# Batch 2's first matmul in seven products, a two-bank end and a searched table of priority shifts in a linear attention plus MLP kernel

## The chip, the cores and the metric

The kernel runs on one core of one Trainium2 chip. The time is the device time of one execution in microseconds. A core has five engines, each with its own instruction queue: TensorE (PE, matmuls; PEld is its weight load), VectorE (DVE), ScalarE (ACT), GpSimd (POOL) and SyncE (SP). Transfers are issued from the queues of SP, POOL and ACT and run on 16 DMA engines. A queue is worked off in its order, so an instruction that waits holds all those behind it.

## What is computed

The reference is a linear attention over 8 batches, 8 heads, 576 positions and head width 64, followed by an MLP with a squared ReLU over all 4608 tokens (512 to 2048 to 512). Inputs and output are float32.

```python
pos = np.arange(S)
theta = np.pi / 2.0 * pos / S
def phi(x, c, s):
    r = np.maximum(x, 0.0)
    return np.concatenate([r * c, r * s], axis=-1)
q_p, k_p = phi(q, cos_w, sin_w), phi(k, cos_w, sin_w)
kv = np.einsum('bhsf,bhsd->bhfd', k_p, v)
z = np.sum(k_p, axis=2)
num = np.einsum('bhsf,bhfd->bhsd', q_p, kv)
den = np.einsum('bhsf,bhf->bhs', q_p, z)[..., None] + 1e-06
x = (num / den).transpose(0, 2, 1, 3).reshape(B * S, H * D)
h = x @ w_in
g = np.maximum(h, 0.0) ** 2
out = g @ w_out
```

## The kernel before

**Batches and tails.** A batch has 576 positions: four groups of 128 (j = 0 to 3, J = 4) and a tail of 64. The MLP works on nine blocks m of 512 tokens: m = 0 to 7 are the four full groups of a batch, and m = 8 holds the eight tails. The first matmul (x times w_in) has 16 row blocks hb of 128 hidden units, the second (g times w_out) sums over them.

**The attention of a batch.** DVE or ACT make the features of k (`plan_k`), cast v (`plan_v`) and make those of q (`plan_q`); L278 and L282 are one such operation on ACT and on DVE, L300 and L302 the casts. PE multiplies k and v into the pair of banks abank (L324), one copy takes that to kvz (L335). The q features are transposed by a DMA that SP issues (L348) or, in batches 0 and 1, by PE (L357). PE makes numerator and denominator (L375), DVE divides (`att_div`, L393 to L399), and the result x is transposed into xT, two groups j at a time, by a DMA of SP (L416) or by PE (L421).

**The seven products.** Both matmuls can be done as a product of 2 x 2 block matrices with seven block products instead of eight, with sums and differences of blocks (the Winograd form). For the second matmul this is so for every batch but the first: sums of w_out's blocks are made once (L665, into w2t), sums of g's blocks per batch (`g_sum`, L684, into gs), and `product` (L705) issues each block product as two halves (sub 0 and 1) of eight matmuls of 256 columns. For the first matmul it is so from batch FIRST_7 on (L1152: 3). There `w1_sum` (L495) makes four sums of w_in's blocks once, w1t; one of them is written over a block of w_in, so it must come behind the last plain matmul. `x_sum` (L519) makes four differences of xT's blocks per batch into the buffers xs; `in_product` (L537) issues a block product as four matmuls of 256 columns. Four lanes u cover the hidden units, alternately on banks 0 and 1 and on banks 2 and 3 (`LANES`, L521). In each lane ACT copies product 5 aside (L933), seeds one bank with the contents of the other (L916, twice) and does two ReLUs (L553), DVE adds product 5 to two results (`in_add`, L560), takes their maximum with zero (L577), and squares the lane (L477).

**The plain first matmul.** In batches 1 and 2 (`plan_gemm1`) each of the 16 hb is four matmuls of 512 columns (L460; for three of batch 1's, L444 in two halves of 256) and one ReLU on ACT (L469); DVE squares four hb at a time (L477). Batch 0 has its own code (L585, L595, L604, L610).

**The order.** `Plan` holds every step from batch 0's first matmul on, with its engine or engines, cost, due time and lag. `order` derives a due time for each step from those that depend on it (L62 to L68), and then fills the engines greedily: each free engine takes, of the steps that are ready in the plan's own clock, the one with the earliest due time (L87). The result is a fixed sequence per engine. A step that lists DVE and ACT is given to either. `plan_load`, `plan_qT` and `plan_x` add the loads and the transposes of SP's queue. The loads of batches 0 and 1 and of the weights stand outside the plan.

**The end.** Block 8's second matmul uses banks 0 (X), 1 (Y), 5 (Z) and 4 (V), L1029. `last` writes a result block to ysb by ACT (L994) or, with product 5 added, by DVE (L990), and `store_half` stores it with two DMAs (L639). The last product, 4, adds onto bank Z; then two ACT copies, one for each half (`last_copy`, L650), and four stores of 64 KB (`put_quarter`, L647), three issued from SP and one from ACT.

Of the kernel before, what the change touches and what calls it, by code (L numbers as in the profile page):

```python
# [13 lines left out]

EPS = 1e-06
FP = 512


class Plan:
# [10 lines left out]
    def add(self, eng, dur, fn, r=(), w=(), due=None, lag=None, name="", after=0.0):  # L30


        n = len(self.ops)
        deps = set()
        for key in r:
            if key in self.last_write:
                deps.add(self.last_write[key])
        for key in w:
            if key in self.last_write:
                deps.add(self.last_write[key])  # L40
            deps.update(self.readers.get(key, ()))
        at = max([self.given.get(key, 0.0) for key in (*r, *w)] + [after])
        for key in r:
            self.readers.setdefault(key, set()).add(n)
        for key in w:
            self.last_write[key] = n
            self.readers[key] = set()
            self.given.pop(key, None)
        if isinstance(eng, str):
            eng, dur, fn = (eng,), (dur,), (lambda e, f=fn: f())  # L50
        lag = self.LAG[eng[0]] if lag is None else lag
        self.ops.append([eng, dur, fn, deps, due, lag, at, name])
        return n

    def order(self, t0):
        ops = self.ops
        n = len(ops)
        after = [[] for _ in range(n)]
        for i, op in enumerate(ops):
            for d in op[3]:  # L60
                after[d].append(i)
        due = [0.0] * n  # L62
        for i in reversed(range(n)):
            eng, dur, _, _, own, lag, _, _ = ops[i]
            t = own if own is not None else 1e6
            for s in after[i]:
                t = min(t, due[s] - min(dur) - lag)
            due[i] = t  # L68
        left = [len(op[3]) for op in ops]
        ready = [op[6] for op in ops]  # L70
        free = {"PE": t0, "ACT": t0, "DVE": t0, "POOL": t0, "SP": t0}
        waiting = {e: [] for e in free}
        for i in range(n):
            if not left[i]:
                for e in ops[i][0]:
                    waiting[e].append(i)
        done, self.by = [], {}
        self.start, self.due = [0.0] * n, due
        while len(done) < n:
            best = None  # L80
            for e, some in waiting.items():
                if some:
                    s = max(free[e], min(ready[i] for i in some))
                    if best is None or s < best[0]:
                        best = (s, e)
            s, e = best
            i = min((i for i in waiting[e] if ready[i] <= s + 0.02), key=lambda i: (due[i], i))  # L87
            s = max(s, ready[i])
            for other in ops[i][0]:
                waiting[other].remove(i)  # L90
            self.by[i] = e
            dur, lag = ops[i][1][ops[i][0].index(e)], ops[i][5]
            free[e] = s + dur
            self.start[i] = s
            done.append(i)
            for a in after[i]:
                left[a] -= 1
                ready[a] = max(ready[a], s + dur + lag)
                if not left[a]:
                    for o in ops[a][0]:  # L100
                        waiting[o].append(a)
        return sorted(done, key=lambda i: (self.start[i], i))
# [7 lines left out]
def kernel(  # L110
# [9 lines left out]
    nc = tc.nc  # L120
# [596 lines left out]
    def half_bank(to):  # L717
        return bank[to][:, :].rearrange("p (s c) -> p s c", s=2)
# [81 lines left out]
    def q_parts(js):  # L800
        return [qp_key(j) + (x,) for j in js for x in "cs"]

    def plan_qT(b, i):
        js = (2 * i, 2 * i + 1) if i < J // 2 else (J,)
        add("SP", 2.0 if i < J // 2 else 1.5, lambda: att_qT(b, i), r=q_parts(js),
            w=[("qpT", i)], lag=CARE + (2.4 if i < J // 2 else 1.7))
        for j in js:
            where[b, j] = ("qpT", i)
# [12 lines left out]
    def x_key(j):  # L821
        return ("xt",) if j == J else ("x", j)
# [6 lines left out]
    def plan_x(b, i):  # L829
        js = (2 * i, 2 * i + 1) if i < J // 2 else (J,)  # L830
        w = [("xT", b % 2, j) for j in js] if i < J // 2 else [("xT8", b // 2)]
        if i < J // 2:
            add("SP", 1.3, lambda: att_x(b, i), r=[x_key(j) for j in js], w=w, lag=1.7 + CARE)
        else:
            add("SP", 1.2, lambda: att_x(b, i), r=[x_key(j) for j in js], w=w, lag=1.7 + CARE)

    def plan_x_pe(b, j, to, due, eng):
        add("PE", 4 * 0.057, lambda: att_x_pe(b, j, to), r=[x_key(j)], w=[("bank", to)], due=due)
# [131 lines left out]
    def plan_gemm2(m, t, dt):  # L970
        hs = range(HB2)
        g = lambda i, j: g_keys(m, i, j, hs)
        s = lambda n: [("gs", n, h) for h in hs]
        reads = {1: g(0, 0), 2: g(0, 1), 5: s(1), 6: s(2), 7: g(1, 0), 3: s(4), 4: g(1, 1)}
        c = [0]

        def prod(n, to):
            for sub in range(2):
                add("PE", 8 * 0.1092, lambda sub=sub: product(m, n, sub, to), r=reads[n] + [("w2t", n, c2) for c2 in range(2)],
                    w=[("bank", to)], due=t + c[0] * dt, name=f"p{m}.{n}.{sub}")  # L980
                c[0] += 1

        def seed(a, b):
            add("ACT", cost("ACT", 512, "psum"), lambda: nc.scalar.copy(out=bank[b][:, :], in_=bank[a][:, :]),
                r=[("bank", a)], w=[("bank", b)])

        def last(a, i, cc, five):
            if five:
                add("DVE", cost("DVE", 512, "psum"),
                    lambda: nc.vector.tensor_tensor(out=y_view(m, i, cc), in0=half_bank(a), in1=five_of(m)[:, :, :], op=ALU.add),  # L990
                    r=[("bank", a), ("five",)], w=[("y", y_slot(m, i), cc)])
            else:
                add("ACT", cost("ACT", 512, "psum"),
                    lambda: nc.scalar.copy(out=y_view(m, i, cc), in_=half_bank(a)),  # L994
                    r=[("bank", a)], w=[("y", y_slot(m, i), cc)])
# [13 lines left out]

        if m < B:  # L1010
            X, Y = 4, 5
            prod(1, X)
            prod(5, Y)
            five(Y)
            seed(X, Y)
            prod(6, Y)
            prod(2, X)
            last(X, 0, 0, False)
            seed(Y, X)
            prod(7, X)  # L1020
            prod(3, Y)
            last(X, 1, 1, True)
            last(Y, 0, 1, True)
            store(0)
            prod(4, X)
            last(X, 1, 0, False)
            store(1)
            return
        X, Y, Z, V = 0, 1, 5, 4  # L1029
        prod(1, X)  # L1030
        seed(X, Y)
        prod(2, X)
        last(X, 0, 0, False)
        store_half(0, 0, ("POOL", "POOL"))
        prod(6, Y)
        seed(Y, Z)
        prod(5, V)
        five(V)
        prod(7, Z)
        last(Z, 1, 1, True)  # L1040
        store_half(1, 1, ("POOL", "POOL"))
        prod(3, Y)
        last(Y, 0, 1, True)
        store_half(0, 1, ("SP", "SP"))
        prod(4, Z)
        for sub in range(2):
            add("ACT", cost("ACT", 256, "psum"), lambda sub=sub: last_copy(sub, Z),
                r=[("bank", Z)], w=[("y", 1, 0, sub)])
            for g, q in enumerate(("SP", "ACT") if sub else ("SP", "SP")):
                add(q, 0.6, lambda g=g, q=q, sub=sub: put_quarter(1, ENG[q], g, sub, 0, DM2),  # L1050
                    r=[("y", 1, 0, sub)], w=[("out", m, 1, 0, g, sub)])

# [96 lines left out]
    t = tB + 4.0  # L1149
    dC = 0.98  # L1150
    win[0] = (t, t + 14.0)
    FIRST_7, STRIDE, SHIFT = 3, 2.0, -6.0  # L1152
    if FIRST_7 == 1:
        plan_w1_sums(28.0)
        plan_gemm1_7(1, t, 0.5)
# [120 lines left out]
```

## Time and profile before

| | |
|---|---|
| median of 3 runs | 281.94 us (280.93 to 282.44) |
| profiled execution | 282.92 us, of which the span is 281.1 us |
| granted TensorE clock | 0.999 |
| HBM read, written | 36.70 MB, 9.44 MB |
| DVE squares L477 | 32 instructions, 38.0 us busy |
| plain ReLUs L469 on ACT | 32 instructions, 18.9 us busy |
| seeds L916 and copies of product 5, L933, on ACT | 48 and 24 instructions, 27.8 and 14.2 us |
| out stores of 512 KB from SP | 16, 4.0 us from issue to landing |

The profile is one execution. Its span goes from the first to the last instruction; 1.8 us of the device time lie around it. PE's instructions overlap in their ends, so where times are added the chain of waits and the distances of starts are used rather than the mean length of one matmul (273 ns for 256 columns, at a distance of 109).

```profile
DVE  1567775899998959698999999998799869949901
ACT  3575962987957875599997997965555553675220
DMA  6999999899999999989999999292033100300224
```

These are the 40 slices of the span: the tenths in which DVE, ACT and the DMA engines were busy. The transfers fill the first 60% of the span and then thin out.

### The profile page before, as it was taken

What the parts mean: (1) busy time and instruction counts of PE and PEld (TensorE: products, weight loads), DVE (VectorE), ACT (ScalarE), POOL (GpSimd) and SP (SyncE); (2) the same over time, 40 slices, a digit from 0 to 9 for tenths busy, and PEclk for the clock granted to TensorE, in tenths of its full rate; (3) what the DMA queues carried; (4) which work ended last, traced back from release to release, by engine and by line L of the source; (5) the groups of instructions that cost most, each with busy time, mean ns of one, the idle gap of its engine ahead of it and who ended that gap; (6) DMA issues with size and microseconds to landing.
All of it is one profiled execution on the core that took longest, in us unless ns stands there. A gap on an engine that the chain in (4) does not pass through costs nothing.

```text
span 281.1 us, 6673 instructions
## 1 busy us (share of the span) xinstructions
PE 267.1 (95%) x2702; PEld 214.5 (76%) x2707; DVE 224.4 (80%) x442; ACT 185.5 (66%) x330; POOL 18.2 (6%) x31
## 2 busy tenths in 40 slices
PE   8599999999799989998999999999999999999993
PEld 3378965565466658897889898998898888888882
DVE  1567775899998959698999999998799869949901
ACT  3575962987957875599997997965555553675220
POOL 8427000000000000000000000000000000000011
PEclk9999999999999999999999999999999999999999
DMA  6999999899999999989999999292033100300224
GB/s 216 312 206 293 315 225 365 234 241 340 280 179 280 256 193 235 332 221 216 323 209 323 201 253 263 43 231 106 2 74 116 55 2 0 152 0 2 111 79 112
DMA packets 83566, 53.38 MB, mean 190 GB/s; under 512 B 55888, under 2 KB 79952, under 8 KB 83536
## 3 DMA queue, kind: packets, MB, share of 16 engines
q1 hardware_dynamic: 77472, 42.41, 58.8%
q0 software_dynamic: 5984, 10.49, 15.8%
q8 instruction: 21, 0.34, 0.5%
q14 instruction: 9, 0.07, 0.1%
q10 hardware_dynamic: 80, 0.07, 0.1%
HBM read 36.70 MB, written 9.44 MB: 164 GB/s over the span
## 4 chain that ended last, share of the span: by engine, by line
PE 79%; DMA 10%; DVE 5%; issue 1%; POOL 1%; SPq 1%; ACT 1%; POOLq 0%; DVEq 0%
PE bank L705 30%; PE bank L537 24%; PE bank L460 6%; PE bank L610 5%; PE bank L585 5%; DMA xT<-x 5%; PE abank L324 3%; DMA q<-in_q_dram 3%; PE abank L375 3%; DMA v<-in_v_dram 2%; PE bank L357 1%; DVE gT L477 1%; SPq L176 1%; PE bank L444 1%; PE bank L421 1%
## 5 line engine op out<-in xcount | busy, mean ns | idle before, releaser
L705 PEld LDWEIGHTS <-gT 128*128 128x128 bf16 x512 | 49.5, 98 | 7.2 <-DVE gT L477 0.3
L705 PE MATMUL bank<-w2sb,gT 128*128 128x256 bf16 x384 | 49.8, 273 | 0.0
L553 ACT ACTIVATE gT<-bank 128x512 bf16<-128x512 f32 x48 | 28.4, 600 | 31.4 <-PE bank L537 30.8
L477 DVE TENSOR_TENSOR gT<-gT 128x2048 bf16<-128x2048 bf16 (+1 forms) x32 | 38.0, 1188 | 7.9 <-ACT gT L553 6.7
L537 PE MATMUL bank<-xT,w1sb 128*128 128x256 bf16 x288 | 42.4, 273 | 1.4 <-DMA xT<-x 1.4
L537 PEld LDWEIGHTS <-w1sb 128*128 128x128 bf16 x384 | 36.8, 98 | 6.6 <-DMA xT<-x 2.0
L705 PEld LDWEIGHTS <-gs 128*128 128x128 bf16 x384 | 37.1, 98 | 6.2 <-DVE gs L684 1.4
L560 DVE TENSOR_TENSOR gT<-bank,qpTp 128x512 bf16<-128x512 f32 x48 | 32.1, 685 | 6.9 <-PE bank L537 5.0
L705 PE MATMUL bank<-w2t,gs 128*128 128x256 bf16 x256 | 33.2, 273 | 0.8 <-DVE gs L684 0.7
L537 PEld LDWEIGHTS <-w1t 128*128 128x128 bf16 x288 | 27.1, 98 | 4.5 <-DVE qpTp L519 1.2
L537 PE MATMUL bank<-qpTp,w1t 128*128 128x256 bf16 x192 | 28.3, 273 | 0.8 <-DVE qpTp L519 0.8
L460 PE MATMUL bank<-xT,w1sb 128*128 128x512 bf16 x116 | 27.8, 379 | 1.3 <-DMA xT<-x 1.3
L916 ACT COPY bank<-bank 128x512 f32<-128x512 f32 x48 | 27.8, 588 | 0.5
L469 ACT ACTIVATE gT<-bank 128x512 bf16<-128x512 f32 x32 | 18.9, 596 | 9.8 <-PE bank L460 9.5
L399 DVE TENSOR_TENSOR x<-abank,rden 128x512 bf16<-128x512 f32 x31 | 21.4, 691 | 1.1
L460 PEld LDWEIGHTS <-w1sb 128*128 128x128 bf16 x116 | 10.5, 98 | 11.5 <-DMA xT<-x 1.6
L639 POOL DMA_DIRECT2D out_dram<-ysb x4 | 2.4, 617 | 245.4 <-ACT ysb L994 242.2
L933 ACT COPY qpTp<-bank 128x512 f32<-128x512 f32 x24 | 14.2, 598 | 5.2 <-PE bank L537 5.0
L705 PE MATMUL bank<-w2sb,gs 128*128 128x256 bf16 x128 | 16.6, 273 | 0.0
L705 PE MATMUL bank<-w2t,gT 128*128 128x256 bf16 x128 | 16.5, 273 | 0.0
L990 DVE TENSOR_TENSOR ysb<-bank,y 128x512 f32<-128x512 f32 x16 | 11.0, 685 | 6.8 <-PE bank L705 6.6
L994 ACT COPY ysb<-bank 128x512 f32<-128x512 f32 x15 | 8.8, 588 | 11.2 <-PE bank L705 10.9
(101 smaller groups left out, 431.7 us busy)
## 6 DMA issues: line engine op xcount, KB each, us to landing
out_dram<-ysb SPq DMA_DIRECT2D x16, 512.0 KB, 4.0
v<-in_v_dram SPq DMA_DIRECT2D x12, 512.0 KB, 6.9
q<-in_q_dram SPq DMA_DIRECT2D x12, 512.0 KB, 5.3
k<-in_k_dram SPq DMA_DIRECT2D x12, 512.0 KB, 6.5
v<-in_v_dram POOLq DMA_DIRECT2D x2, 1024.0 KB, 12.6
w1sb<-in_moe_w_in_dram POOLq DMA_DIRECT2D x4, 512.0 KB, 12.7
w2sb<-in_moe_w_out_dram POOLq DMA_DIRECT2D x4, 512.0 KB, 15.3
k<-in_k_dram SPq DMA_DIRECT2D x1, 1024.0 KB, 5.4
```

What stands on the lines that cost most here:

```text
L399: nc.vector.tensor_tensor(out=x[:, a:z], in0=n4[:, :, :, 0:D].rearrange("p b (k l) d -> p b k l d", l=2), in1=rden[:, a:z] .rearrange("p b ...
L460: nc.tensor.matmul(out=out_, lhsT=w1sb[:, kb, hb * P : (hb + 1) * P], rhs=x_block(m, kb), start=(kb == 0), stop=(kb == KB - 1),)
L469: nc.scalar.activation(out=gT_of(m)[:, hb, :], in_=bank[to][:, :], func=ACTF.Relu)
L477: nc.vector.tensor_tensor(out=g, in0=g, in1=g, op=ALU.mult)
L537: nc.tensor.matmul(out=bank[to][:, s * W : (s + 1) * W], lhsT=lhs[:, kb, (2 * u + s) * P : (2 * u + s + 1) * P], rhs=rhs[:, kb, :], start= ...
L553: nc.scalar.activation(out=g_pair(m, i, j, u), in_=bank[to][:, :].rearrange("p (s c) -> p s c", s=2), func=ACTF.Relu,)
L560: nc.vector.tensor_tensor(out=g_pair(m, i, j, u), in0=bank[to][:, :].rearrange("p (s c) -> p s c", s=2), in1=in_five(u).rearrange("p (s c) ...
L585: nc.tensor.matmul(out=bank[2 * (s % 2) + i // 2][:, i % 2 * W + c : i % 2 * W + c + step], lhsT=w1sb[:, kb, hb * P : (hb + 1) * P], rhs=x ...
L610: nc.tensor.matmul(out=bank[FIRST_Y[tt]][:, :], lhsT=gT_of(0)[:, hb, tt * P : (tt + 1) * P], rhs=w2sb[:, hb, :], start=(hb == 0), stop=(hb ...
L705: nc.tensor.matmul(out=bank[to][:, s * DM2 : (s + 1) * DM2], lhsT=lhs[:, hb, s * P : (s + 1) * P], rhs=rhs[:, hb, :], start=(fresh and hb ...
L916: add("ACT", psum, lambda: nc.scalar.copy(out=bank[b][:, :], in_=bank[a][:, :]), r=[("bank", a)], w=[("bank", b)])
L933: add("ACT", psum, lambda u=u, Y=Y: nc.scalar.copy(out=in_five(u), in_=bank[Y][:, :]), r=[("bank", Y)], w=five)
```

## The change

Three things are changed.

1. FIRST_7 goes from 3 to 2: batch 2's first matmul is done in seven products, and w_in's block sums (`plan_w1_sums`) may start from the plan's time 28 on.
2. In the end of block 8, bank Z is copied by ACT in two halves into banks 2 and 3 after product 7. The first half of product 4 adds onto bank 2 and the second onto bank 3. Each half is copied to ysb and stored when it is done: the first by two stores from POOL, the second by one from SP and one from ACT.
3. The planner adds a number from the table SHIFTS (306 entries, from -12.6 to 12.8) to the due time of a step, by the step's number. Between two steps that only PE can do, the lag is taken as zero (`behind`). The costs of four of SP's transposes in the plan are raised.

```diff
+SHIFTS = {
+    40: -2.8, 60: -2, 72: -3.8, 74: -2.4, 78: 4, 92: -1.2, 126: -1.4, 137: 1.2, 145: 7.4, 147: 2.2,
...
+    1128: 0.2, 1130: -4.8, 1131: -1.4, 1137: -1.6, 1139: 0.2, 1140: -2, 1194: 1, 1199: -7.6,
+}
...
+    def behind(self, i, a):
+
+        return 0.0 if self.ops[i][0] == self.ops[a][0] == ("PE",) else self.ops[i][5]
+
     def order(self, t0):
...
             for s in after[i]:
-                t = min(t, due[s] - min(dur) - lag)
-            due[i] = t
+                t = min(t, due[s] - min(dur) - self.behind(i, s))
+            due[i] = t + SHIFTS.get(i, 0.0)
...
-                ready[a] = max(ready[a], s + dur + lag)
+                ready[a] = max(ready[a], s + dur + self.behind(i, a))
...
-        add("SP", 2.0 if i < J // 2 else 1.5, lambda: att_qT(b, i), r=q_parts(js),
+        add("SP", 2.3 if i < J // 2 else 1.6, lambda: att_qT(b, i), r=q_parts(js),
             w=[("qpT", i)], lag=CARE + (2.4 if i < J // 2 else 1.7))
...
-            add("SP", 1.3, lambda: att_x(b, i), r=[x_key(j) for j in js], w=w, lag=1.7 + CARE)
+            add("SP", 1.7, lambda: att_x(b, i), r=[x_key(j) for j in js], w=w, lag=1.6 + CARE)
         else:
-            add("SP", 1.2, lambda: att_x(b, i), r=[x_key(j) for j in js], w=w, lag=1.7 + CARE)
+            add("SP", 1.4, lambda: att_x(b, i), r=[x_key(j) for j in js], w=w, lag=1.7 + CARE)
...
         prod(7, Z)
         last(Z, 1, 1, True)
         store_half(1, 1, ("POOL", "POOL"))
+
+        for sub in range(2):
+            add("ACT", cost("ACT", 256, "psum"),
+                lambda sub=sub: nc.scalar.copy(out=half_bank(2 + sub)[:, sub, :], in_=half_bank(Z)[:, sub, :]),
+                r=[("bank", Z)], w=[("bank", 2 + sub)])
         prod(3, Y)
         last(Y, 0, 1, True)
         store_half(0, 1, ("SP", "SP"))
-        prod(4, Z)
         for sub in range(2):
-            add("ACT", cost("ACT", 256, "psum"), lambda sub=sub: last_copy(sub, Z),
-                r=[("bank", Z)], w=[("y", 1, 0, sub)])
-            for g, q in enumerate(("SP", "ACT") if sub else ("SP", "SP")):
+            add("PE", 8 * 0.1092, lambda sub=sub: product(m, 4, sub, 2 + sub), r=reads[4] + [("w2t", 4, c2) for c2 in range(2)],
+                w=[("bank", 2 + sub)], due=t + c[0] * dt, name=f"p{m}.4.{sub}")
+            c[0] += 1
+            add("ACT", cost("ACT", 256, "psum"), lambda sub=sub: last_copy(sub, 2 + sub),
+                r=[("bank", 2 + sub)], w=[("y", 1, 0, sub)])
+            for g, q in enumerate(("SP", "ACT") if sub else ("POOL", "POOL")):
                 add(q, 0.6, lambda g=g, q=q, sub=sub: put_quarter(1, ENG[q], g, sub, 0, DM2),
                     r=[("y", 1, 0, sub)], w=[("out", m, 1, 0, g, sub)])
...
-    FIRST_7, STRIDE, SHIFT = 3, 2.0, -6.0
+    FIRST_7, STRIDE, SHIFT = 2, 2.0, -6.0
```

More of the change, by code (lines that the diff above doesn't have):

```diff
@@ L63, in order @@
         for i in reversed(range(n)):
-            eng, dur, _, _, own, lag, _, _ = ops[i]
+            _, dur, _, _, own, _, _, _ = ops[i]
             t = own if own is not None else 1e6
             for s in after[i]:
-                t = min(t, due[s] - min(dur) - lag)
-            due[i] = t
+                t = min(t, due[s] - min(dur) - self.behind(i, s))
+            due[i] = t + SHIFTS.get(i, 0.0)
         left = [len(op[3]) for op in ops]
@@ L91, in order @@
             self.by[i] = e
-            dur, lag = ops[i][1][ops[i][0].index(e)], ops[i][5]
+            dur = ops[i][1][ops[i][0].index(e)]
             free[e] = s + dur
```

32 rows, old and new, of the table SHIFTS are left out of this document.

## The prediction

> **What bounds the kernel now.** I read the busy shares first, then the same by stage, then what TensorE (PE) waited for, then the last microseconds.
>
> ```profile
> PE 267.1 (95%) x2702; PEld 214.5 (76%) x2707; DVE 224.4 (80%) x442; ACT 185.5 (66%) x330; POOL 18.2 (6%) x31
> L460 PE MATMUL bank<-xT,w1sb 128*128 128x512 bf16 x116 | 27.8, 379 | 1.3 <-DMA xT<-x 1.3
> ...
> L560 DVE TENSOR_TENSOR gT<-bank,qpTp 128x512 bf16<-128x512 f32 x48 | 32.1, 685 | 6.9 <-PE bank L537 5.0
> ```
>
> PE is busy for 95% of the span. The L460 row is the plain first matmul in 512-wide pieces: 64 of its 116 are batch 2's, which the change replaces; the L560 row is one of the vector operations that seven products bring along.
>
> ```profile
> core 0: us, PE busy (x) PEld busy (x) DVE busy (x) ACT busy (x) POOL busy (x), PEclk, DMA share, GB/s
> 36.00:55.00 19.00, 18.79 (x172) 10.79 (x174) 12.99 (x33) 10.94 (x20) 0.00 (x0) 1.00 1.01 267
> 55.00:70.00 15.00, 15.00 (x140) 8.59 (x138) 14.65 (x30) 11.59 (x21) 0.00 (x0) 1.00 1.07 296
> 70.00:84.00 14.00, 11.99 (x119) 7.61 (x118) 13.61 (x28) 10.48 (x20) 0.00 (x0) 1.00 1.09 233
> 84.00:112.00 28.00, 26.54 (x249) 18.96 (x247) 23.46 (x47) 20.60 (x37) 0.00 (x0) 1.00 1.09 243
> 112.00:140.00 28.00, 27.09 (x312) 23.85 (x311) 24.02 (x48) 23.91 (x44) 0.00 (x0) 1.00 0.95 268
> 140.00:168.00 28.00, 28.00 (x302) 24.85 (x300) 27.16 (x55) 25.15 (x46) 0.00 (x0) 1.00 1.10 253
> 168.00:196.00 28.00, 28.00 (x321) 25.16 (x319) 26.74 (x53) 19.61 (x37) 0.00 (x0) 1.00 0.67 162
> ```
>
> Columns after the stretch: its length, then the busy time of each engine. PE is full in 55:70 and from 140 on. From 70 to 140 it stands still for 2.01, 1.46 and 0.91 us. VectorE (DVE) is nearly full in 55:84 (28.3 of 29), but only at 84% in 84:112.
>
> ```profile
> PE bank L537 <- DMA xT<-x: 1.4, 2, 0.9
> PE bank L460 <- DMA xT<-x: 1.3, 1, 1.3
> PE bank L537 <- DVE qpTp L519: 0.8, 1, 0.8
> PE bank L705 <- DVE gs L684: 0.7, 1, 0.7
> ```
>
> These are the waits behind the idle time: late transposed inputs xT, and late DVE sums (gs, and the input differences of L519).
>
> ```profile
> 103.56 0.61 PE L537 MATMUL bank<-qpTp,w1t 128*128 128x256 bf16 x4 [0.75 <-DVE qpTp L519]
> ```
>
> This is the first product of batch 3 that needs an input difference; it is my mark for how far each kernel has come.
>
> ```profile
> 274.58 1.91 PE L705 MATMUL bank<-w2t,gT 128*128 128x256 bf16 x16
> 276.52 0.65 ACT L650 COPY ysb<-bank 128x256 f32<-128x256 f32 x2 [4.78 <-PE bank L705]
> 276.92 1.78 SPq L647 DMA_DIRECT2D out_dram<-ysb  x3
> 277.20 0.56 ACTq L647 DMA_DIRECT2D out_dram<-ysb  x1
> ```
>
> The last product ends at about 276.49; then two ACT copies, four small stores, and the end at 281.1.
>
> **The base.** The sum is made against the profiled execution: 282.92 us, of which 281.1 are the span and 1.8 lie around it. It stands 0.98 above the median of the runs, 281.94. I carry a change of the span onto that median.
>
> **Batch 2 in seven products, on PE.** 64 matmuls of 512 columns become 112 of 256. In the chain of waits four of the first kind take 0.865 us, eight of the second 0.873: 64 x 0.216 = 13.83 against 112 x 0.109 = 12.23, so -1.6.
>
> Every 256-wide matmul also needs its weight load, of which there are 48 more. The loads' mean is 98 ns, yet the last 128 matmuls of the chain take 14.11 us, 110 ns each, so they lie wholly beside the matmuls. The Trainium skill (TensorE: Matmul & The Clock Gate, The mechanism) says that loads overlap matmuls only where row groups differ; all these use all 128 rows, so by that rule 48 x 0.098 = 4.7 us would be added and the part would cost 3.1. The trace disagrees.
>
> **On ACT and DVE.** Batch 2's sixteen ACT relus (L469, about 0.6) become eight relus, eight seed copies (L916) and four copies of product 5 (L933): +4 x 0.6 = 2.4 us on an engine at 20.6 of 28; hidden. DVE gets eight L560 (starts 0.61 apart), four maxima (0.35) and four L519 (0.34): +7.6 us. The four weight sums of L495 (1.13 each), which stood between 81.7 and 106.3, go forward: in the built order one stands behind the squares at about 27, two about the v casts at 39 to 41. DVE was idle 1.08 us up to 28.6 and 4.34 us up to 44.9, so these three cost nothing; without that cover they would cost 3.4. The fourth must wait for the last plain unit of batch 1 and lands at about 73, where DVE has no slack. As cover, several feature operations (0.40 each) go from DVE to ACT: between the sums of batch 1 and those of batch 2, DVE has 13 features and casts where it had 19.
>
> **DVE up to batch 1's sums.** In the old kernel the second half of the first sum (L684) is done at 73.16. The new order puts before it one more feature (0.40) and the fourth weight sum (1.13), and takes out a cast (0.34): +1.2. The attention matmuls of batch 1, which these wait for, stand behind about 0.6 us more of L610 work: 75.0. PE had product 1 of batch 1 finished at 71.99, and now does 0.87 of batch 2 before it needs the sum: 72.9, a wait of 2.1. Before it waited 0.71 + 1.31 = 2.02 here. A wash, but the place has a new owner: DVE in place of the transposed input.
>
> That input is not gone. In the old queue two 512 KB stores stood ahead of its second half, which was issued at 70.11 and landed 5.9 us later. Now the stores follow it and one v load precedes it. With 3.5 us (the median of these transposes) to 5.9 us it lands 74.2 to 76.6, counted from 70.7; its difference is wanted at 75.0. Cost 0 to 1.6, I take 0.5. Behind it on DVE all four differences queue, and with them six of the seven products.
>
> **From there to the mark.** DVE's list from 75.0 through the first difference of batch 3, by the distances of starts in its timeline: seven feature operations 2.8; three casts 1.0; five attention divisions 5.2 (1.04 each); eight L560 4.9; four maxima 1.4; four squares of 2048 4.6; eight half sums L684 4.8; two output sums 1.2; five differences 1.7: 27.6. PE after its wait has 3.1 of work up to batch 2's second products (78.1), then 200 matmuls of 256 and 88 of 65 columns (0.0306 each), 24.5, so 102.6: DVE decides. It is never quite full. In 140:196, where the same mix runs, its share is 53.9 of 56, 96%: 27.6 / 0.96 = 28.75, and the mark is reached at 103.75. Before: 103.56. But behind the mark the old order has 1460 matmuls of 256 and 320 of 65, the new 1432 and 320. So 28 x 0.109 - 0.2 = 2.9 us gained: the 1.6, and the old PE's waits of 0.60 (at 98.4, for batch 3's xT) and 0.75 (at the mark itself), which a PE that arrives with DVE does not have.
>
> **Behind the mark.** Old idle time there: 0.85 (xT, at 129) and 0.13. The whole order is new, and each new neighbourhood can open a wait; in 140:262 there was none to win. Bounds: -1.0 (those two gone) to +1.5 (as much as 84:112 shows, once). I take +0.7.
>
> **The end.** L650's two copies waited for all 16 matmuls of product 4; now the first follows the first eight and only one copy (0.375) is behind the last. Before, SP issued its third quarter store at 278.2, 1.71 after the product's end; the new last ones, from SP and ACT, start 0.03 + 0.375 + 0.03 = 0.44 after it: -1.27. POOL's two (0.62 each to issue) begin 0.4 before the product's end, the second 0.2 after; its stores took 2.3 to 3.1 us to land against 2.3 of SP's: at worst the gain is 0.7. New are two ACT copies that seed the banks, about 0.65, behind product 7 and beside product 3 (1.75); if they come after DVE's read of that bank (0.75) the cover is 0.15. I take -1.0, bounds -0.7 to -1.3.
>
> For POOL's stores the Trainium skill (DMA: Bandwidth & Descriptors, Anatomy of one DMA) has 2.0 us plus bytes / 436e3, for 64 KB an estimate of 2.15; with that the end would gain 1.15. No row here shows a 64 KB store from POOL.
>
> **Sum.** -2.9 + 0.5 + 0.7 - 1.0 = -2.7: 281.94 - 2.7 = 279.2 us. The planner's other edits (no lag between two PE steps, longer costs of SP's transposes) add no instruction; they act through the order alone.
>
> **Rivals.** *Everything fits* (0.15): no new wait behind the mark, none for xT, PE rather than DVE reaches the mark, 1.1 earlier: -2.9 - 1.1 - 1.0 - 1.0 = -6.0, 275.9. For it: the idle time is there to be filled. Against: DVE was never over 98% in any stage.
>
> *DVE with small gaps* (0.13): 90% in place of 96% gives 27.6 / 0.90 = 30.7, +1.9: 281.1. For it: 84:112 and 112:140 ran at 84 and 86%, though they partly waited for DMA.
>
> *DMA sets the pace* (0.10): its share is 0.95 to 1.10 up to 168. If batch 4's xT still lands at 129.4, the 2.9 turns into waiting there and only the end stays: 280.9. Against: the chain shows these transposes released by DVE's division.
>
> *DVE becomes the bound* (0.19), the one on the other side: between 75 and 104 DVE and PE wait for each other in turn (division for attention matmul, product for a bank that L560 reads). At the 84% of the old 84:112 the list takes 32.9: +4.1, so 283.3, and with xT and later waits at their upper bounds 285.2; call it 284.2. It decides from a share under 88%, where 2.7 is used up. For it: 7.6 us more DVE work in a stage without cover. Against: the stretches 55:84 and 140:196 hold 96 to 97%.
>
> *Weight loads are not hidden* (0.01), by the loads' mean of 98 ns: -2.7 + 4.7, 283.9; every 256-wide row speaks against it.
>
> **How the numbers follow.** The forecast has 0.42; its own range, from its bounds without all of them at one end, is 277.6 to 280.9. Over 0.5% (1.4 us, about what a measurement of this kernel can tell from no change) faster: 0.36 of it, 0.15, and 0.07 of the two middle rivals: 0.58. Slower: 0.16 of the fourth and 0.02: 0.18. The rest, 0.24, is the same. The range reaches down most of the way to the first rival and up into the fourth: 276.8 to 283.6.
>
> **What would show it.** PE's waits: a DVE wait of about 2 us for gs near 73 and at most 0.5 for xT; no L495 among them. DVE at 95% or more from 75 to 104, and batch 3's first difference product at 102.6 to 104.5. After the last product one ACT copy and about 3.6 us to the end, not 4.6. Wrong, if PE waits over 2 us in total behind 140, if DVE falls below 88% between 75 and 104, or if the seeds hold up product 4.

## The result and the profile after

| | before | after |
|---|---|---|
| median | 282.19 us (280.93 to 283.53, 4 runs) | 278.99 us (278.64 to 279.47, 4 runs) |
| profiled execution | 282.92 us, span 281.1 | 279.47 us, span 277.7 |

The ratio is 0.988, with a 95% interval of 0.983 to 0.992: 3.2 us faster. The forecast was 279.2. (Ratios here and below leave disturbed runs out, while medians don't; in e4 below, with three such runs of six, the two therefore differ.)

The lines of the changed kernel stand 43 further down: L705, L537, L519, L495 and L684 are now L748, L580, L562, L538 and L727. First PE, DVE and the others by stage, with the columns of before:

```profile
core 0: us, PE busy (x) PEld busy (x) DVE busy (x) ACT busy (x) POOL busy (x), PEclk, DMA share, GB/s
70.00:84.00 14.00, 11.87 (x139) 9.28 (x137) 13.90 (x29) 14.00 (x26) 0.00 (x0) 1.00 0.93 233
84.00:112.00 28.00, 26.54 (x300) 23.42 (x299) 25.97 (x53) 25.08 (x46) 0.00 (x0) 1.00 1.11 232
112.00:140.00 28.00, 28.00 (x313) 25.23 (x313) 26.48 (x54) 22.49 (x41) 0.00 (x0) 1.00 1.03 246
```

PE still stands still for 2.13 us in 70:84 (2.01 before) and for the same 1.46 us in 84:112. Only the 0.91 us of 112:140 are gone. What it waited for (the waits of PE: total, times, longest):

```profile
PE bank L748 <- DVE gs L727: 1.9, 1, 1.9
PE bank L580 <- DMA xT<-x: 1.5, 1, 1.5
```

The first is the new wait for batch 1's sums, the second is again a transposed input, now batch 3's first half. In PE's timeline it stands ahead of the product of 98.87, and the mark, the first product of batch 3 that takes a difference, follows at 105.63:

```profile
98.87 0.61 PE L580 MATMUL bank<-xT,w1sb 128*128 128x256 bf16 x4 [1.46 <-DMA xT<-x]
...
105.63 0.60 PE L580 MATMUL bank<-qpTp,w1t 128*128 128x256 bf16 x4
```

DVE between the sums of batch 1 and the mark (same columns as the stages): 27.44 of 29 us, 95%. Its first difference for batch 3 starts at 104.06.

```profile
75.00:104.00 29.00, 27.00 (x314) 23.27 (x315) 27.44 (x57) 26.39 (x49) 0.00 (x0) 1.00 1.06 240
```

The end, in the timeline: the two seeds, product 4 in its two banks, the first copy while the second half runs, POOL's two stores, the second copy, the last two stores.

```profile
270.31 0.63 ACT L1088 COPY bank<-bank 128x256 f32<-128x256 f32 x2 [1.07 <-DVE ysb L1033]
...
271.08 1.91 PE L748 MATMUL bank<-w2t,gT 128*128 128x256 bf16 x16
...
272.15 0.37 ACT L693 COPY ysb<-bank 128x256 f32<-128x256 f32 x1 [1.20 <-PE bank L748]
272.81 1.07 POOL L690 DMA_DIRECT2D out_dram<-ysb  x2 [1.04 <-ACT ysb L693]
273.02 0.37 ACT L693 COPY ysb<-bank 128x256 f32<-128x256 f32 x1 [0.50 <-PE bank L748]
273.43 0.56 ACTq L690 DMA_DIRECT2D out_dram<-ysb  x1
273.43 0.56 SPq L690 DMA_DIRECT2D out_dram<-ysb  x1
```

The order is as described: the seeds finish at 270.94, before product 4; one copy and one store per queue follow the last product, which ends at 272.99. Yet from there to the end of the span pass 4.7 us. Before it was 281.1 - 276.49 = 4.6. (Below, the end is counted from the start of the last matmul plus 0.11, the distance of two matmuls; that gives 0.2 more for both.)

### The profile page after: what moved, and what is told of

Same layout as the page of the kernel before. It is cut to its first block, busy times and chain, and to the rows that moved or that the text cites. A ratio compares the mean times of both kernels' runs of the same rounds, so it can differ in the third digit from the quotient of the medians.

```text
span 277.7 us, 6808 instructions
## 1 busy us (share of the span) xinstructions
PE 266.2 (96%) x2755; PEld 220.3 (79%) x2755; DVE 228.6 (82%) x452; ACT 190.3 (69%) x342; POOL 19.2 (7%) x33
## 4 chain that ended last, share of the span: by engine, by line
PE 83%; DMA 5%; DVE 4%; ACT 4%; POOL 1%; issue 1%; POOLq 0%; ACTq 0%; DVEq 0%
PE bank L748 33%; PE bank L580 30%; PE bank L628 4%; PE bank L653 4%; PE bank L503 3%; PE abank L367 3%; PE abank L418 3%; DMA q<-in_q_dram 3%; DMA xT<-x 3%; PE bank L400 1%; ACT qp L321 1%; ACT kp L321 1%; DVE x L442 1%; DVE qp L325 1%; DVE kp L325 1%
## 5 line engine op out<-in xcount | busy, mean ns | idle before, releaser
L748 PEld LDWEIGHTS <-gT 128*128 128x128 bf16 x512 | 49.6, 98 | 6.2
L596 ACT ACTIVATE gT<-bank 128x512 bf16<-128x512 f32 x56 | 33.3, 602 | 26.2 <-PE bank L580 26.1
L580 PE MATMUL bank<-xT,w1sb 128*128 128x256 bf16 x336 | 48.6, 273 | 1.7 <-DMA xT<-x 1.5
L580 PEld LDWEIGHTS <-w1sb 128*128 128x128 bf16 x448 | 43.0, 98 | 7.2 <-DMA xT<-x 1.7
L748 PE MATMUL bank<-w2sb,gT 128*128 128x256 bf16 x384 | 48.0, 273 | 0.0
L603 DVE TENSOR_TENSOR gT<-bank,qpTp 128x512 bf16<-128x512 f32 x56 | 36.3, 684 | 8.6 <-PE bank L580 7.9
L748 PEld LDWEIGHTS <-gs 128*128 128x128 bf16 x384 | 36.8, 98 | 6.7 <-DVE gs L727 2.4
L580 PEld LDWEIGHTS <-w1t 128*128 128x128 bf16 x336 | 32.0, 98 | 3.6
L748 PE MATMUL bank<-w2t,gs 128*128 128x256 bf16 x256 | 32.4, 273 | 1.9 <-DVE gs L727 1.9
L580 PE MATMUL bank<-qpTp,w1t 128*128 128x256 bf16 x224 | 32.5, 273 | 0.0
L580 PE MATMUL bank<-xT,w1t 128*128 128x256 bf16 x112 | 16.6, 273 | 0.0
L321 ACT ACTIVATE kp<-k,sin_col 128x512 bf16<-128x512 f32 x22 | 15.5, 720 | 1.5 <-DMA k<-in_k_dram 1.5
L580 PE MATMUL bank<-zeros,w1sb 128*128 128x256 bf16 x112 | 16.3, 273 | 0.0
L748 PE MATMUL bank<-w2t,gT 128*128 128x256 bf16 x128 | 16.1, 273 | 0.0
L748 PE MATMUL bank<-w2sb,gs 128*128 128x256 bf16 x128 | 16.1, 273 | 0.0
L628 PE MATMUL bank<-xT,w1sb 128*128 128x256 bf16 (+1 forms) x160 | 15.2, 251 | 0.0
```

The source lines that it names most:

```text
L321: eng.activation(out=dst[ps, :, lo : lo + D], in_=src[ps], func=ACTF.Relu, scale=col[ps])
L580: nc.tensor.matmul(out=bank[to][:, s * W : (s + 1) * W], lhsT=lhs[:, kb, (2 * u + s) * P : (2 * u + s + 1) * P], rhs=rhs[:, kb, :], start= ...
L596: nc.scalar.activation(out=g_pair(m, i, j, u), in_=bank[to][:, :].rearrange("p (s c) -> p s c", s=2), func=ACTF.Relu,)
L603: nc.vector.tensor_tensor(out=g_pair(m, i, j, u), in0=bank[to][:, :].rearrange("p (s c) -> p s c", s=2), in1=in_five(u).rearrange("p (s c) ...
L628: nc.tensor.matmul(out=bank[2 * (s % 2) + i // 2][:, i % 2 * W + c : i % 2 * W + c + step], lhsT=w1sb[:, kb, hb * P : (hb + 1) * P], rhs=x ...
L748: nc.tensor.matmul(out=bank[to][:, s * DM2 : (s + 1) * DM2], lhsT=lhs[:, hb, s * P : (s + 1) * P], rhs=rhs[:, hb, :], start=(fresh and hb ...
```

## The experiments

Twelve variants, each with runs of the kernel before on the same chip beside it. The table has the median, the ratio to before with its interval, the time of the profiled execution, and where PE stood still in that execution (stage length less PE's busy time).

| variant | median us | ratio | profiled us | idle 20:70 | 70:84 | 84:112 | 112:140 | 140:250 |
|---|---|---|---|---|---|---|---|---|
| before | 282.19 | 1 | 282.92 | 0.56 | 2.01 | 1.46 | 0.91 | 0.00 |
| after | 278.99 | 0.988 (0.983, 0.992) | 279.47 | 0.72 | 2.13 | 1.46 | 0.00 | 0.00 |
| e1 after, old end | 279.02 | 0.989 (0.986, 0.992) | 278.87 | 0.72 | 2.14 | 0.95 | 0.00 | 0.00 |
| e2 before, new end | 283.02 | 1.002 (0.999, 1.005) | 280.96 | 0.34 | 1.72 | 0.41 | 0.00 | 0.59 |
| e3 after, empty table | 282.09 | 1.001 (0.998, 1.004) | 283.00 | 0.35 | 2.76 | 0.95 | 1.93 | 0.00 |
| e4 before, batch 2 in seven | 288.11 | 1.014 (1.006, 1.021) | 285.81 | 1.99 | 0.92 | 2.25 | 2.76 | 0.00 |
| e5 before, both planner edits | 279.16 | 0.989 (0.986, 0.992) | 278.74 | 0.59 | 1.48 | 0.02 | 0.00 | 0.00 |
| e7 after, v load moved | 278.59 | 0.986 (0.982, 0.990) | 278.04 | 0.72 | 1.85 | 0.00 | 0.00 | 0.00 |
| e9 table, early entries | 281.52 | 0.997 (0.994, 1.000) | 281.21 | 1.76 | 2.37 | 0.04 | 0.41 | 0.12 |
| e10 table, late entries | 285.31 | 1.012 (1.008, 1.016) | 283.25 | 0.56 | 3.13 | 2.00 | 0.00 | 1.10 |
| e11 before, no PE lag | 282.77 | 1.000 (0.997, 1.002) | 281.73 | 0.85 | 1.99 | 1.17 | 0.00 | 0.00 |
| e12 before, SP costs | 279.60 | 0.988 (0.984, 0.991) | 278.02 | 0.56 | 1.10 | 0.00 | 0.00 | 0.03 |
| e13 e7, end without POOL | 278.25 | 0.984 (0.980, 0.988) | 277.89 | 0.98 | 2.14 | 0.00 | 0.00 | 0.00 |
| e14 e3, no squares | 281.67 | 0.996 (0.994, 0.999) | 280.04 | 0.61 | 2.93 | 0.00 | 0.40 | 0.00 |

The before rows of the four groups had medians from 282.2 to 282.8. A profiled execution can lie a microsecond or two off its kernel's median (e2, e4, e10 and e14 above all), so the stages show where, and the medians how much.

**The end alone (e1, e2).** The block of the end (the diff's third part from `prod(7, Z)` on) is exchanged, all else stays.

> The changed kernel with the old end: product 4 onto bank Z in one piece, both copies behind it, three 64 KB stores from SP and one from ACT. All instructions before the end stand in the same order. Theory of the forecast (the end is worth 1.0 us): time 1.0 us above the changed kernel, near 280.0, and 5.6 us or more from the last matmul to the end of the span. Theory after the two traces (the end is worth nothing, since the span ran on for 4.6 us after the last matmul before the change and for 4.7 after it): time within 0.4 us of the changed kernel's 279.0, and about 4.6 us from the last matmul to the end.

> The kernel before with the new end alone. Theory of the forecast: 1.0 us faster than before, ratio 0.9965, and 3.6 us from the last matmul to the end of the span. Theory that the end is worth nothing: ratio 1.000 within its interval, 4.6 to 4.8 us from the last matmul to the end, with POOL's closing drain ending last as in the changed kernel (1.4 us behind its last packet).

With the old end the changed kernel takes the same time, and the old kernel gains nothing by the new end. From the last matmul's start plus 0.11 to the end of the span the traces have 4.81 us before, 4.87 after, 4.87 in e1 and 4.83 in e2. The end is worth nothing.

**Seven products alone, and the table alone (e3, e4).**

```diff
-SHIFTS = {
...
-}
+SHIFTS = {}
```

```diff
-    FIRST_7, STRIDE, SHIFT = 3, 2.0, -6.0
+    FIRST_7, STRIDE, SHIFT = 2, 2.0, -6.0
```

> The changed kernel with an empty table: seven products in batch 2, the new end, the planner's other edits. If the table brings most of the gain (theory A: it filled about 2 us of idle TensorE time, above all behind 104 us), TensorE waits 2 us or more longer than in the changed kernel and the time is 281 or above. If the 1.6 us less TensorE work brings the gain and the table next to nothing (theory B), it is 279 to 279.5.

> The kernel before with FIRST_7 = 2 alone: the old planner orders seven products in batch 2. Theory B (the work itself): 1.6 us faster than before, ratio 0.994. Theory A (work saved in a stage where VectorE and the transfers are late is not time saved until the order is made for it): ratio 0.998 to 1.02, and VectorE near full from 70 to 112 us with TensorE waiting for the sums of L495, L519 and L684 there.

Without the table the changed kernel is as slow as before, and batch 2's seven products in the old planner cost 1.4%. Both times are theory A's. (A part of the 1.4% can be the clock: among the runs behind that ratio the granted clock was 0.990, 0.994 and 1.000, and the times 285.8, 287.8 and 284.0.) What PE waited for in e4:

```profile
PE bank L537 <- DVE qpTp L519: 3.4, 2, 2.8
PE bank L537 <- DMA xT<-x: 2.4, 2, 1.4
```

and in e3, where the lines have other numbers (L545 is the seven products of the first matmul, L713 those of the second):

```profile
PE bank L545 <- DVE qpTp L527: 1.7, 3, 1.2
PE bank L545 <- DMA xT<-x: 1.4, 2, 0.7
PE bank L713 <- DVE gs L692: 1.4, 1, 1.4
```

Both wait for differences and for the transposed inputs from which these are made. So far it looked as if the table made the gain. The next group says otherwise.

**The planner's edits alone (e5, e11, e12).** e5 is the kernel before with `behind` and SP's new costs, FIRST_7 = 3, the old end, no table. e11 has only `behind`, e12 only the costs:

```diff
-        add("SP", 2.0 if i < J // 2 else 1.5, lambda: att_qT(b, i), r=q_parts(js),
+        add("SP", 2.3 if i < J // 2 else 1.6, lambda: att_qT(b, i), r=q_parts(js),
...
-            add("SP", 1.3, lambda: att_x(b, i), r=[x_key(j) for j in js], w=w, lag=1.7 + CARE)
+            add("SP", 1.7, lambda: att_x(b, i), r=[x_key(j) for j in js], w=w, lag=1.6 + CARE)
...
-            add("SP", 1.2, lambda: att_x(b, i), r=[x_key(j) for j in js], w=w, lag=1.7 + CARE)
+            add("SP", 1.4, lambda: att_x(b, i), r=[x_key(j) for j in js], w=w, lag=1.7 + CARE)
```

> The kernel before with the planner's two edits alone (no lag between two PE steps, longer costs of SP's transposes): batch 2 stays plain, the old end, an empty table. Theory A (these edits only change what the planner believes; without a table the order they give is as good as the old one): 281.5 to 282.9 us, the same as before. Rival B (they repair the order by themselves; without them seven products cost 288.1, with them 282.1): clearly below before, 280.0 to 281.3.

> Of the two planner edits only the first (no lag between two steps of PE); SP's old costs, batch 2 plain, the old end, an empty table. With both edits it was 279.16 us. Theory A (the lag edit carries it: the planner no longer believes that PE must pause 0.31 us between two of its own dependent products, and so stops pushing other PE work in between): 278.8 to 280.0 us. Rival B (the longer costs of SP's transposes carry it, because the order of loads and transposes on the queue is what changed): 281.5 to 283.0. Rival C (neither by itself; any new order is a new draw, worth up to 3 us either way): anywhere in 279 to 286, with no relation to the two together.

> Of the two planner edits only the second (SP's transposes planned 0.2 to 0.4 us longer); the lag as before, batch 2 plain, the old end, an empty table. Theory A (the lag edit carries the gain): 281.5 to 283.0 us. Rival B (these costs carry it): 278.8 to 280.0. Rival C (each new order is a new draw): anywhere in 279 to 286.

Three cost lines (the first of the two for xT also shortens a lag by 0.1), without any of the three things that the change is named for, give the whole gain: 0.988 in e12 as in the changed kernel. The lag edit alone gives none. e11 and e12 both came out as rival B has it; e5, at 279.16, came out below even its rival B (280.0 to 281.3).

That any new order is a new draw, rival C, is not excluded, since the new costs were tried with one set of values. What speaks against it is a third pair of kernels: e3 differs from e4 by both planner edits and the new end, which is worth nothing, and there too the kernel with the new costs is the better one, 1.001 against 1.014.

The stages of e12:

```profile
70.00:84.00 14.00, 12.90 (x130) 8.49 (x128) 13.93 (x27) 10.77 (x20) 0.00 (x0) 1.00 1.05 242
84.00:112.00 28.00, 28.00 (x281) 21.16 (x279) 25.41 (x50) 21.26 (x39) 0.00 (x0) 1.00 1.12 260
112.00:140.00 28.00, 28.00 (x313) 25.05 (x312) 25.92 (x53) 24.09 (x44) 0.00 (x0) 1.00 1.08 260
```

PE is full from 84 to 140, where it stood still for 2.37 us before. Its waits between 60 and 250 us are only these; none is for xT:

```profile
PE bank L713 <- DVE gs L692: 0.7, 1, 0.7
PE abank L332 <- DVE xt L407: 0.4, 1, 0.4
```

Why was xT late before? The second division of batch 3, the last that its first transpose needs, ended at 91.03 (its start 90.34 and 0.69). SP's timeline before, then that of e12 (start, length of issue, queue and line, operation):

```profile
84.36 2.17 SPq L176 DMA_DIRECT2D q<-in_q_dram  x2
86.57 0.51 SPq L176 DMA_DIRECT2D k<-in_k_dram  x1
87.18 1.00 SPq L176 DMA_DIRECT2D v<-in_v_dram  x2
88.29 4.25 SPq L348 DMA_TRANSPOSE qptT<-qpt  x1
92.58 0.63 SPq L186 DMA_DIRECT2D kt<-in_k_dram  x1
93.31 2.12 SPq L416 DMA_TRANSPOSE xT<-x  x1
...
99.75 1.25 SPq L416 DMA_TRANSPOSE xT<-x  x1
```

```profile
86.55 1.24 SPq L356 DMA_TRANSPOSE qptT<-qpt  x1
87.83 0.74 SPq L184 DMA_DIRECT2D v<-in_v_dram  x1
89.61 1.24 SPq L424 DMA_TRANSPOSE xT<-x  x1
...
94.21 2.56 SPq L424 DMA_TRANSPOSE xT<-x  x1
```

Before, five loads of 512 KB were issued from 84.36 on; the transpose of the tails' q features behind them took 4.25 us to issue, where the same issue took 1.24 in e12, with three such loads under way ahead of it instead of five. So batch 3's inputs, ready at 91.03, were issued at 93.31. In e12 that transpose comes ahead of the v loads, the division ends at 89.58, and the inputs go out at 89.61.

The second half, which the mark needs, was held up longer. Its last division ended at 95.22 (94.53 and 0.69), but loads of the tails and the tails' own transpose stood ahead of it on SP, and it was issued at 99.75. DVE's first difference waited for it:

```profile
103.08 0.43 DVE L519 TENSOR_TENSOR qpTp<-xT 128x512 bf16<-128x512 bf16 x1 [2.91 <-DMA xT<-x]
```

In e12 that division ended at 94.18, and the transpose was issued at 94.21.

e12 reaches the mark at 100.43, before at 103.56. Up to there PE's order is the same in both, so its lead can be followed matmul by matmul. It is 0.5 us from about 16 us on, because the first q load landed sooner (12.54 against 13.05). At the three waits for transposed inputs before (76.09, 98.97, and 103.56 by way of DVE's difference) it grows by 1.5, 0.8 and 0.9; in between, e12 loses 0.55 at 79.61. That makes 3.1. The orders of DVE and ACT change in e12 too, from 71 us on, so this run doesn't show that SP's queue alone does it; e7 tests one transfer by itself.

**Parts of the table (e9, e10).** The 66 entries of steps planned to start before 100 us, and the other 240.

> The changed kernel with only those 66 entries of the table whose steps are planned to start before 100 us; up to there the order is the changed kernel's, behind it the planner's own. Theory A (the table's gain is made where the kernel without it waits for differences and transposed inputs, 104 to 140; its lead at 140 was 2.3 us under the changed kernel's, at 96 nothing): it reaches the mark like the changed kernel (105.2 to 106.0) and then loses, 280.8 to 282.3 us. Rival B (the table's early part makes the gain, for instance the weight sums and batch 1's sums): 278.7 to 279.8 us.

> The changed kernel with only those 240 entries of the table whose steps are planned to start at 100 us or later; the order before is the planner's own. Theory A (as for the early half: the gain is made behind 100): 279.0 to 280.4 us, most of the gain kept. Rival B (the early part makes it): 281.2 to 282.8 us. Rival C (the late entries only fit the order they were searched with, so that alone they are random shifts): slower than the kernel without a table, over 282.8 us.

Neither half works alone, and the late one is 3.2 us slower than no table at all: rival C. e9's time lies in the range of its theory A, but it doesn't speak for that theory, since one thing that the expectation says is not so: a shift also moves the due times of all steps ahead of it in its chain, so the order up to 100 is not the changed kernel's in e9 (1.76 us idle in 20:70 against 0.72). The halves are not clean parts, and the place of the table's gain stays open. What they show fits numbers that suit one order only.

**One transfer (e7).** In the changed kernel SP issued 512 KB of batch 4's v between batch 3's division, which ended at 90.75, and its transpose:

```profile
88.30 1.13 SPq L219 DMA_DIRECT2D q<-in_q_dram  x2
89.47 0.62 SPq L229 DMA_DIRECT2D vt<-in_v_dram  x1
90.14 1.50 SPq L219 DMA_DIRECT2D v<-in_v_dram  x1
91.75 3.36 SPq L459 DMA_TRANSPOSE xT<-x  x1
```

The variant changes the emission key of that one step, so that it goes behind the transpose:

```diff
-        return sorted(done, key=lambda i: (self.start[i], i))
+        return sorted(done, key=lambda i: (self.start[i] + (1.63 if i == 490 else 0), i))
```

> The changed kernel with one transfer moved: SP issues the first half of batch 4's v load behind the transpose of batch 3's first inputs instead of ahead of it; no other engine's order changes. Theory A (DMA sets the pace there: the transpose is issued at 91.75 and lands at 98.87 because 512 KB of v stand ahead of it, and PE waits 1.46 us for it): it is issued at about 90.8, lands by 97.7, PE's wait falls under 0.6, PE reaches the first difference product of batch 3 at 104.1 to 104.9 instead of 105.63, and the time falls by 0.5 to 1.2: 277.8 to 278.5 us. Rival B (the queue's bytes ahead of it are the two q loads, or what PE gains is lost to DVE, which reaches the mark at 104.06): landing or mark as before within 0.4, and 278.6 to 279.3 us.

```profile
90.70 1.27 SPq L459 DMA_TRANSPOSE xT<-x  x1
92.01 1.80 SPq L219 DMA_DIRECT2D v<-in_v_dram  x2
```

```profile
97.37 0.60 PE L580 MATMUL bank<-xT,w1sb 128*128 128x256 bf16 x4
...
104.12 1.04 PE L580 MATMUL bank<-qpTp,w1t 128*128 128x256 bf16 x8
```

The division ends at 90.64 here, and the transpose goes out 1.05 us earlier than in the changed kernel. It lands 4.1 us after its issue (94.77) in place of 7.1 (98.83). PE's wait for it is gone, the products behind it start at 97.37 in place of 98.87, and the mark is reached at 104.12, 1.5 earlier. The mechanism is theory A's. DVE's first difference, due at 104.06 in the changed kernel, starts at 102.88 and did not hold PE up here. The Trainium skill (DMA: Bandwidth & Descriptors, Queues, rings and completion order) says that each DMA engine takes up the descriptors of one queue in their order; the trace agrees, since with 512 KB less ahead of it the transpose landed 4.1 us sooner. The time of the profiled execution fell by 1.4 us, but the median by only 0.4, just outside the range of theory A: three of the six runs lie at 277.0 to 278.0, three at 279.1 to 279.3. The two intervals overlap, so that it beats the changed kernel is likely and not shown.

Two things beside the edit lie in that profiled execution, and they nearly cancel. Its first q load landed 0.9 us sooner than in the changed kernel (11.80 against 12.74). Against that, the granted clock (the first number behind POOL's two) fell to a mean of 0.60 between 75 and 79 us:

```profile
75.00:79.00 4.00, 4.00 (x34) 2.87 (x35) 3.27 (x11) 3.56 (x7) 0.00 (x0) 0.60 0.94 241
```

Matmuls of 256 columns stood 0.21 us apart there in place of 0.11. From 79.25 up to the transposed inputs e7 is 0.1 us behind the changed kernel, so its lead at the mark does come from this one wait. The granted clock can have a part in the small gain of the median: in the three longer runs it was 0.989 to 0.994, in the two shortest 0.998 and 1.000.

**The end without POOL's stores (e13).** On top of e7, SP issues the first half's two stores.

```diff
-            for g, q in enumerate(("SP", "ACT") if sub else ("POOL", "POOL")):
+            for g, q in enumerate(("SP", "ACT") if sub else ("SP", "SP")):
```

> The kernel with the v load behind the transpose (278.59 us), and at the end SP issues the first half's two quarter stores in place of POOL. Theory A (POOL's closing wait of 3.7 us, from its last stores, holds up the end): from the last product to the end 4.3 to 4.6 us in place of 4.95, and 278.0 to 278.4 us. Rival B (the end goes by the last stores' landing and the closing waits of SP, wherever the stores are issued; SP now issues four one behind the other): 4.7 to 5.2 us, and 278.4 to 278.9 us.

```profile
271.45 0.37 ACT L693 COPY ysb<-bank 128x256 f32<-128x256 f32 x1 [0.50 <-PE bank L748]
271.85 0.56 ACTq L690 DMA_DIRECT2D out_dram<-ysb  x1
271.85 1.84 SPq L690 DMA_DIRECT2D out_dram<-ysb  x3
```

SP now issues three stores from 271.85 to 273.69, one behind the other, and the end is as long as ever: 4.87 us (4.95 in e7). By this length it is rival B. The time, 278.25, lies in theory A's range, but its ratio's interval overlaps with e7's, and the end shows no gain to account for it. It is the lowest median of all.

**Less DVE work (e14).** In the kernel without a table, batch 2's four squares are left out.

```diff
-                add("DVE", 1.14, lambda u=u: square(m, u, False), w=
+                add("DVE", 1.14, (lambda: None) if m == 2 else (lambda u=u: square(m, u, False)), w=
```

> The changed kernel with the empty table (282.09 us), and batch 2's four squares (1.15 us each on VectorE, about 84 to 100) left out: batch 2 then uses the unsquared activations, and the order of all other instructions stays. Theory A (without the table seven products make VectorE the bound between 75 and 104: its differences come late to PE by 3 x 0.6 us, and one sum by 1.4): the waits for differences up to 104 go and the time falls by 1 to 2.5, to 279.6 to 281.1 us. Rival B (VectorE is late only because transposed inputs and seeds reach it late): the time stays within 0.7 of 282.1. Rival C (the whole loss against the same planner with a plain batch 2, 2.9 us, is VectorE's): 279.0 to 279.5 us.

```profile
84.00:112.00 28.00, 28.00 (x318) 24.72 (x316) 23.31 (x52) 24.86 (x45) 0.00 (x0) 1.00 1.15 245
112.00:140.00 28.00, 27.60 (x307) 24.36 (x305) 25.25 (x51) 24.21 (x44) 0.00 (x0) 1.00 1.09 250
```

The median falls by 0.4, 281.67 against 282.09: rival B by the bounds set, with intervals that overlap. In the profiled execution, the fastest of its twelve, PE is full in 84:112 and the waits for xT are gone there as well, as the divisions come earlier. PE still waits 1.6 us for batch 1's sums. So 4.6 us less on DVE buy at most a part of the 2.9 us by which seven products are slower than e5 under the same planner without a table. What the rest is, stays open.

## Why the prediction was right, and where it was wrong

The total was right, the account of it was not. The gain up to the mark was put too high by 1.9 us and that of the end by 1.0, the gain behind the mark too low by 3.2, and xT's cost too high by 0.5. That these errors add up to less than one microsecond is luck.

**The step that failed: "The planner's other edits ... add no instruction; they act through the order alone."** That gave them no term in the sum; they came in only through the finished order from which the other terms were read. By themselves the costs of SP's transposes are worth 1.2% (e12), as much as the whole change. The seven products, the end and the table together add nothing that can be measured to it: 0.989 in e5, 0.988 after. The old kernel's waits of 0.60 and 0.75, which the forecast credited to the order of seven products, go in e12 without seven products.

**The rival put aside wrongly: "DMA sets the pace."** It had 0.10, because the chain shows the transposes released by DVE's division. The chain names the last releaser. The 2.28 us between the division's end and the issue stood in SP's own timeline, in the 4.25 us of the transpose ahead, and so did the 4.5 us of the second half. It was looked for at batch 4 only, where the wait did go; in the changed kernel it was batch 3 that waited, above all because the transpose, issued 1.0 us after its division, landed only 7.1 us after its issue.

**The mark, -2.9, was -1.0.** DVE's part was right: first difference at 104.06, forecast 103.75, at a share of 95% (forecast 96). But PE came later than DVE, at 105.63, after waiting 1.46 for batch 3's xT, whose landing, 98.83, had hardly moved (before 98.92). By matmuls left at distance times count, 166.2 us of work were left at 105.63, and before 169.2 at 103.56. With the wait taken out, e7 is at the mark 1.5 earlier, 2.5 ahead of before, near the forecast.

**Behind the mark, +0.7, was -2.5.** From the mark to the last product the changed kernel takes 167.2 us for 166.2 of work; before it took 172.8 for 169.2. No new neighbourhood opened a wait, and the old ones there went: the wait for batch 4's xT at 129.4, in which 1.0 us was lost by the distances of starts, and several stalls of 0.1 to 0.3. The bound of -1.0 took only the idle time that the profile counts.

**The end, -1.0, was 0.** The last stores are issued 1.2 us sooner after the last product, at +0.60 in place of +1.83, but their last packet lands only 0.44 sooner, at +3.05 in place of +3.49 (the forecast took landing as a fixed length behind the issue). Then POOL's closing drain, the last wait of its queue, which begins at +0.42 beside the issue of its second store, lasts 3.68 us, to +4.10; SP's is done at +3.92. The rest, to +4.87, follows in every kernel. The last rows of the chain of waits are POOL's store and POOL's queue at the closing line:

```profile
266.00 6.13 PE bank L748 x56
...
272.81 0.54 POOL out_dram L690
273.35 0.53 POOLq L1321
```

Without POOL's stores at the end (e13) POOL's drain is over at +1.90, but SP's last store lands at +3.56 and SP's closing waits end at +4.12: as long. The Trainium skill (DMA: Bandwidth & Descriptors, Issuing engines are not separate DMA queues) says that issuing from several engines saves only the time of the issue; of 1.2 us of issue saved the landing shows 0.44, and the span none.

**xT's second half, +0.5, was 0.** It was issued at 70.83 and had landed when DVE reached its difference at 75.76.

**What held.** The weight sums hide where it was said, since no wait names L538. The new wait for batch 1's sums is 1.9 us (forecast 2.1), with DVE as its owner, "a wash" against 2.01 before. The seeds of the end came in time. The weight loads are hidden: in the chain above 56 matmuls of 256 columns take 6.13 us, 109 ns each, beside loads of 98 ns. And two profiled executions fit the 1.6 us of PE work saved: e13 and e12 have the same span, 276.1 and 276.2, though PE stands still for 3.12 us in the one and 1.69 in the other between 20 and 250. In the changed kernel, as it is, the waits for the sums and for xT eat that saving: PE stands still for 4.31 us there, and for 2.09 in e5.

## What to carry to other kernels

Leave no edit of a planner's costs without a term: build it alone, and compare the queues that it reorders. For a transfer that comes late, compare the end of the work that makes its data with its issue in the queue's own timeline; the chain names the producer even when the queue held it up for 2 us more. A gain in issue time at the end of a kernel counts only as far as the last landing and each engine's closing wait move with it.

## What the runs showed of the hardware

- A transpose's issue on SP took 1.23 us with nothing of SP's under way ahead of it (196.79 in the changed kernel), and 4.52 us (83.73, behind three loads and a store) or 4.25 (88.29 before, behind five loads). SP issued nothing else meanwhile. It isn't the count of transfers alone: behind three loads it took 1.24 in e12.
- POOL's closing drain took 3.68 us after two stores of 64 KB, though these landed by 2.3 us after its start. It took 3.96 us in the kernel before and 3.73 in e13, where it begins 1.1 and 1.8 us ahead of the end of the last product and holds nothing up.
- The kernel before spread by 3.9 us from run to run (281.1 to 285.0 in the 23 runs beside e11 to e14), the changed one by 0.8 (278.6 to 279.5, in 4 runs). Why isn't shown. The granted clock isn't enough: those of the 23 runs with 0.998 or more still lie between 281.2 and 284.0. The landing of the first q load, with which the chain begins, lay between 11.8 us (e7) and 13.05 (before) in the profiles.
- The granted clock was 0.60 from 75 to 79 us in e7, behind a wait of PE of 1.67 us; in the changed kernel it stayed at 1.00 behind a wait of 1.89 at the same place. What decides this isn't shown.
- PE's idle time as the profile counts it misses up to 0.16 us for each stall, since a 256-column matmul is shown as 273 ns long at a distance of 109.
